# Unread products under the first loads, and half of the first key sum moved to VectorE

## The chip, the cores and the metric

The kernel runs on one core of one Trainium2 chip. What counts is the device time of one execution, from launch to the last output row, in microseconds. The core has a matrix engine (TensorE, PE in the rows), three engines for elementwise work (VectorE = DVE, ScalarE = ACT, GpSimd = POOL) and a queue engine (SyncE = SP) that issues most transfers. Each engine runs its own list of instructions strictly in the order in which the program wrote them and waits on the others through semaphores.

## The reference

Attention over 64 heads with pooled queries, then a capacity-limited expert layer whose tokens are assigned greedily by the gate's scores. Cut to what matters:

```python
def _attn_ref(q, k, v):                       # 8 x 8 heads, 1152 keys of 64
    q_pool = q.reshape(B, H, S // 2, 2, D).mean(axis=3)
    scores = scale * np.matmul(q_pool, k.transpose(0, 1, 3, 2))
    scores = scores - np.max(scores, axis=-1, keepdims=True)
    attn = np.exp(scores)
    attn = attn / (np.sum(attn, axis=-1, keepdims=True) + 1e-09)
    return np.matmul(attn, v)
def _moe_ref(x, w_gate, w1, w2):              # 4608 tokens, 8 experts
    order = np.argsort(-(x @ w_gate).flatten())
    ...                                       # each token to one expert, 576 per expert
    out[mask] = np.maximum(x[mask] @ w1[e], 0.0) @ w2[e]
```

## The kernel before

**Tiling.** Two heads make a pair, 32 pairs in all. For a pair the kernel loads keys (`KD`), queries (`QD`, later `QS`) and values (`VD`) in float32 and splits each into a high and a low float16 part (`KH`/`KL`, `QH`/`QL`, `V16`). The scaling of the split comes from a bound: sums of absolute values per partition (`VM`), added over partitions by TensorE into the bank `mb` (line 537 and after), turned into powers of two by VectorE (`VE`, lines 553 and 555) and into factors by ScalarE (`SC`, `EX`).

Ahead of a pair's exponentials its exact row maxima are needed. TensorE multiplies `QH` with `KH` in chunks (line 684 for the first pair, 693 for later ones) and VectorE reduces each chunk to its maximum (line 687, 696). For the first pair this is done head by head: 15 chunks of 384 keys per head, on five PSUM banks for the first head (`ma`, `av0`, `av1`, the first banks of `sc0` and `sc1`) and on `ma` and `mb` for the second. The maxima are folded (lines 724, 725), transposed by TensorE (line 738) and written as an extra row of `QB` by VectorE (lines 742, 745). Only then can the score products of that head start.

A step of attention (`step`, line 759) takes one head and 128 keys: four score products (line 776) into `sc0` or `sc1`, the exponential by ScalarE into `P` (779), the low part `PM` by GpSimd or VectorE (783), and 15 weighted-value products (793). A pair has 18 steps. After the last pair the expert stage follows; the change doesn't touch it.

**Start of the program.** Transfers of the first two pairs are issued at once. TensorE begins with products of two constant tiles (`ones` and `wide`, 128x128 by 128x512, line 916) that nobody reads: 10 into `av1` (key `wu`) and 13 into `av0` (key `wx`).

**What sets the order.** All attention work is collected as items with engine, function, reads and writes; `Cycle.plan` (line 165) emits an item as soon as all that it needs is emitted, always the one with the smallest due time. Due times are a table by tag and pair: `TAU0` for the first pair, `TAU1` and `TAU2` for the next two, `TAU` for the rest. An engine's list is the order in which its items are emitted.

The lines that the steps below touch: `bounds` (522), where `abk` are the absolute sums of the two key halves of the first pair and `vs` the sums by TensorE; `split` (583); `max_chunk` (674); `fill` and `pads` (483, 496), which clear buffers; and the loop over `wu`, `wv`, `wx`, `wy` (914).

Of the kernel before, what the change touches and what calls it, by code (L numbers as in the profile page):

```python
# [21 lines left out]
AF = mybir.ActivationFunctionType  # L22
OP = mybir.AluOpType
AX = mybir.AxisListType
# [3 lines left out]
M = S // 2  # L28
# [124 lines left out]
class Cycle(Order):  # L153
# [11 lines left out]
    def plan(self):  # L165
# [52 lines left out]
TAU0 = {"abk": [-158.8971, -154.1632], "abs": [-18.36343, -4.432959], "aug": [-83.38275, -166.4732], "augt":  # L218
# [5 lines left out]
        -31.28967, -16.54009, 11.37296, -165.2382, 7.395536, -8.984111, -4.211814], "expb": [-29.09149,  # L224
        -22.94875, -1.956318, -58.58073, -17.31112, 8.70511, -44.15053, -10.60943, -83.61574], "fill":
# [150 lines left out]
def attention(ctx, tc, top, kt, qt, v, wg, w1, x_dram, L, npair=NPAIR):  # L376
    nc = tc.nc
    const = ctx.enter_context(tc.tile_pool(name="att_const", bufs=1))
    psum = ctx.enter_context(tc.tile_pool(name="att_psum", bufs=1, space=PSUM))
    od = Cycle()  # L380
# [7 lines left out]
    ones = const.tile([128, 128], BF, name="ones")  # L388
# [1287 lines left out]
```

## Time and profile before

| what | value |
|---|---|
| runs | 1231.44, 1232.99, 1235.9 us; median 1232.99 |
| the profiled execution | 1237.53 us; span of the trace 1235.8 us |
| busy in the span | PE 1190.0 us (96%), DVE 1018.7 (82%), ACT 972.0 (79%), POOL 901.6 (73%) |
| chain that ended last | PE 77%, DVE 13%, DMA 4%, issue 2%, ACT 2% |

Between the execution's time and its span lie 1.7 us of launch and end. A share of the whole span is an average over stages: the first 24 us, the attention of 32 pairs, the routing and the experts have different limits, and a stage has to be read by itself. In timelines the records of neighbouring products overlap, because the end of a product is modelled; a row with a count gives the time from the first start to the last end.

### The profile page before, as it was taken

The page shows a single profiled execution, that of the slowest core. Times are in us where ns is not written, and L with a number is a line of the kernel's source. Part 1 is how long each engine was busy: PE and PEld are TensorE (multiplying, and loading weights), DVE is VectorE, ACT ScalarE, POOL GpSimd, SP SyncE. Part 2 cuts the span into 40 slices and gives each one's busy share as a digit, 9 for nine tenths or more (in the row PEclk, how much of TensorE's full clock was granted, in tenths as well). Part 3 has the DMA queues.
Part 4 walks back from the last instruction along what each step waited for, and adds up shares of the span by engine and source line. Part 5 has one row for each costly group of instructions (what it writes and reads, how often), then busy time and mean ns, then how long its engine had stood idle before and what let it go on. Part 6 is the DMA issues. An engine that isn't in the chain of part 4 may idle for free.

```text
span 1235.8 us, 38902 instructions
## 1 busy us (share of the span) xinstructions
PE 1190.0 (96%) x15470; PEld 860.7 (70%) x15470; DVE 1018.7 (82%) x2743; ACT 972.0 (79%) x1719; POOL 901.6 (73%) x879
## 2 busy tenths in 40 slices
PE   7899999999999999999999999789999999999998
PEld 2567778778778777777787788465657466575673
DVE  6899899999999999999999995779888898893520
ACT  6979899999899898999999986065876686786751
POOL 6978898898888998888888887044775584675641
PEclk9999999999999999999999999889999999999999
DMA  8666776876776866776876730042453554547401
GB/s 250 151 158 165 186 189 163 196 186 160 191 185 160 193 182 162 195 184 159 197 188 157 180 93 20 20 175 86 129 196 111 159 192 130 171 138 230 120 31 39
DMA packets 131218, 190.83 MB, mean 154 GB/s; under 512 B 50268, under 2 KB 86108, under 8 KB 128732
## 3 DMA queue, kind: packets, MB, share of 16 engines
q1 hardware_dynamic: 117948, 126.75, 38.9%
q0 software_dynamic: 12944, 61.58, 17.5%
q8 instruction: 121, 1.98, 0.7%
q14 instruction: 61, 0.50, 0.1%
q10 hardware_dynamic: 144, 0.02, 0.0%
HBM read 116.41 MB, written 18.87 MB: 109 GB/s over the span
## 4 chain that ended last, share of the span: by engine, by line
PE 77%; DVE 13%; DMA 4%; issue 2%; ACT 2%; POOL 0%; SPq 0%; POOLq 0%; ACTq 0%; DVEq 0%
PE sc L776 20%; PE av L793 18%; PE ph L1561 11%; PE po L1591 11%; PE mb L693 4%; PE ma L693 4%; DVE MX L696 3%; PE av L828 1%; DMA BD<-QH 1%; PE av L840 1%; ACT P L779 1%; DMA W<-in_w_dram,widx 1%; PE po L1597 1%; PE rt L1194 1%; DVE HX L1570 1%
## 5 line engine op out<-in xcount | busy, mean ns | idle before, releaser
L783 POOL TENSOR_TENSOR PM<-P 128x576 f16<-128x576 f32 x508 | 612.4, 1266 | 99.6 <-ACT P L779 48.3
L779 ACT ACTIVATE P<-sc,EX 128x576 f32<-128x576 f32 x576 | 412.6, 739 | 76.0 <-PE sc L776 58.8
L793 PEld LDWEIGHTS <-P 128*128 128x128 bf16 x5760 | 293.0, 98 | 30.0 <-issue 1.9
L793 PE MATMUL av<-V,P 128*128 128x65 f16 (+1 forms) x5760 | 301.2, 192 | 0.0
L793 PE MATMUL av<-V,PM 128*128 128x65 f16 x2880 | 292.8, 194 | 0.0
L793 PEld LDWEIGHTS <-PM 128*128 128x128 f16 x2880 | 263.8, 97 | 0.0
L776 PE MATMUL sc<-QA,KA 128*128 128x288 f16 x1152 | 234.5, 285 | 1.4 <-ACT P L779 1.3
L776 PE MATMUL sc<-QB,KB 65*128 65x288 f16 (+1 forms) x1152 | 235.7, 285 | 0.0
L696 DVE TENSOR_REDUCE MX<-mb 128x1 f32<-128x512 f32 x279 | 190.7, 684 | 27.8 <-PE mb L693 22.7
L696 DVE TENSOR_REDUCE MX<-ma 128x1 f32<-128x512 f32 x279 | 190.6, 683 | 9.8 <-PE ma L693 6.8
L776 PEld LDWEIGHTS <-KA 128*128 128x128 f16 x1152 | 106.2, 97 | 73.1 <-issue 22.7
L1591 PE MATMUL po<-W2H,HX 128*128 128x512 f16 x512 | 155.5, 379 | 0.0
L1561 PE MATMUL ph<-XH,W1H 128*128 128x320 f16 (+1 forms) x512 | 146.2, 286 | 0.7 <-DVE WE L1539 0.3
L1561 PE MATMUL ph<-XL,W1H 128*128 128x320 f16 (+1 forms) x512 | 146.2, 286 | 0.6 <-DVE XL L1455 0.6
L1561 PE MATMUL ph<-XH,W1L 128*128 128x320 f16 (+1 forms) x512 | 145.9, 286 | 0.0
L776 PEld LDWEIGHTS <-KB 65*128 65x128 f16 (+1 forms) x1152 | 112.5, 98 | 29.4
L1591 PEld LDWEIGHTS <-HX 128*128 128x128 f16 x768 | 71.2, 98 | 78.5 <-issue 0.5
L1561 PEld LDWEIGHTS <-W1H 128*128 128x128 f16 x1024 | 97.9, 98 | 30.7 <-issue 6.1
L1613 POOL DMA_INDIRECT out_dram<-OT,idx x40 | 39.2, 980 | 109.1 <-ACT OT L1593 91.2
L693 PE MATMUL ma<-KH,BD 128*128 128x512 f16 x279 | 105.7, 379 | 3.5 <-DVE MX L696 1.3
L693 PE MATMUL mb<-KH,BD 128*128 128x512 f16 x279 | 105.5, 378 | 3.3 <-DVE MX L696 1.4
L1514 POOL TENSOR_TENSOR W2L<-W,W2H 128x512 f16<-128x512 f32 x64 | 73.2, 1159 | 38.5 <-ACT W L1512 34.1
(308 smaller groups left out, 2157.9 us busy)
## 6 DMA issues: line engine op xcount, KB each, us to landing
KD<-in_kt_dram SPq DMA_DIRECT2D x64, 288.0 KB
VD<-in_v_dram SPq DMA_DIRECT2D x32, 576.0 KB
WB<-in_w_dram SPq DMA_DIRECT2D x32, 512.0 KB
QA<-QH SPq DMA_DIRECT2D x128, 72.0 KB
KB<-KH SPq DMA_DIRECT2D x64, 144.0 KB
KA<-KH SPq DMA_DIRECT2D x64, 144.0 KB
KA<-KL SPq DMA_DIRECT2D x64, 144.0 KB
x_dram<-X SPq DMA_DIRECT2D x16, 576.0 KB
```

The costliest lines, as they stand in the source:

```text
L693: od.add(t, "PE", 214, lambda: nc.tensor.matmul(m, BD[i][:, j, :], KH[i][:, 512 * c:512 * c + 512], start=True, stop=True), r=bd + [("KH", ...
L696: od.add(t, "DVE", 597, lambda: nc.vector.tensor_reduce(MX[i][:, j, c:c + 1], m, axis=AX.X, op=OP.max), r=[mk], w=[("MX", i, j, c)], tag=" ...
L776: nc.tensor.matmul(c[:, t, :288], a[i][:rows, s, ks], b[i][:rows, s, 288 * t:288 * t + 288], start=first, stop=not first)
L779: od.add(g + 0.1, "ACT", 624, lambda: nc.scalar.activation(p.rearrange("p (t q) -> p t q", t=2), c[:, :, :288], AF.Exp, scale=EX[n % 3][:, ...
L783: od.add(g + 0.2, en, dur, lock=1, fn=lambda: eng.tensor_tensor(pm, p, hi, op=OP.subtract), r=[("P32", g % NP)], w=[("PM", g % NM)], tag="pm")
L793: nc.tensor.matmul(out, w[:, qs], v, start=kb == 0 and j == 0 and y == 0, stop=kb == NKB - 1 and y == 2, skip_group_check=True)
L828: nc.tensor.transpose(m[:, 128 * z:128 * z + 128], X[u][:, 3 * q + z], ident)
L840: nc.tensor.matmul(av[1][32 * q:32 * q + E, :384], wgs[:, c], XT[q].rearrange("p c t -> p (c t)"), start=True, stop=True)
L1514: od.add(tt, "POOL", 1230, lambda o=lo[p], a=raw[p], h=hi[p]: nc.gpsimd.tensor_tensor(o, a, h, op=OP.subtract), r=[key, hk, sk], w=[(nm + ...
L1561: nc.tensor.matmul(p, a[:, d, fs], b[:, d, qs], start=z == 0, stop=z == 11)
L1591: nc.tensor.matmul(o, a[:, z, q0:q0 + 128], b[:, z], start=z == 0 and y == 0, stop=z == 7 and y == 2)
L1613: st = nc.gpsimd.indirect_dma_start(out=out, out_offset=bass.IndirectOffsetOnAxis(ap=idx[i][:n, c:c + 1], axis=0), in_=OT[ob][:n], in_offs ...
```

## The change

Four edits, and new due times for the first three pairs.

1. The 13 unread products `wx` go; `wu` grows from 10 to 11 and is due before all else.
2. Behind the sums of the first pair's bound stand six unread products into `av1` (tag `wv`).
3. Behind 12 of the 15 chunk products of the first head stands one unread product into the second bank of `sc0`.
4. The absolute sum of the second key half of the first pair is a VectorE reduce (tag `abd`) in place of a ScalarE activation with accumulation.

The core of the diff:

```diff
-TAU0 = {"abk": [-158.8971, -154.1632], ..., "wu": [-17.875, -17.555, ...], "wx": [-4.689, -4.369, ...], ...}
+TAU0 = {"abd": [-140.0], "abk": [-3.247596, -6.270317], ..., "wu": [-300, -299.99, ...], "wv": [-250], ...}
...
-      5, "np": 10, "nm": 10, "stick": 1, "nx": 3, "wu": 10, "pd": [4, 12], "wv": 0, "pd0": [], "pd1": [1, 2, 4, 9, 10,
-      15, 16, 17], "d1": 2.0, "cw1": 0.7, "wx": 13, "wy": 0}
+      5, "np": 10, "nm": 10, "stick": 1, "nx": 3, "wu": 11, "pd": [4, 12], "wv": 0, "pd0": [], "pd1": [1, 2, 4, 9, 10,
+      15, 16, 17], "d1": 2.0, "cw1": 0.7, "wx": 0, "wy": 0}
...
         if n == 0 and not a:
-            for z in range(2):
-                od.add(t, "ACT", 680, lambda z=z: nc.scalar.activation(
-                    VJ[:, :M], KD[n % 2][:, z * M:z * M + M], AF.Abs, accum_out=VM[i][:, 3 * z:3 * z + 1]), ..., tag="abk")
+            od.add(t, "ACT", 680, lambda: nc.scalar.activation(
+                VJ[:, :M], KD[0][:, :M], AF.Abs, accum_out=VM[i][:, 0:1]), r=[("KD", 0, 0)], w=[("VM", i, 0)], tag="abk")
+            od.add(t, "DVE", 680, lambda: nc.vector.tensor_reduce(VM[i][:, 3:4], KD[0][:, M:2 * M], axis=AX.X, op=OP.add, apply_absolute_value=True),
+                   r=[("KD", 0, 1)], w=[("VM", i, 3)], tag="abd")
...
+        if not n and not a:
+            def busy():
+                for _ in range(6):
+                    nc.tensor.matmul(av[1], ones, wide, start=True, stop=True)
+            od.add(t + AT["bs"], "PE", 1280, busy, r=["mb"], w=["av1"], tag="wv")
...
-            od.add(t, "PE", 163, lambda: nc.tensor.matmul(
-                m[:q, :384], QH[i][r, 128 * j:128 * j + q], KH[i][r, 384 * c:384 * c + 384], start=True, stop=True),
-                r=..., w=[mk], tag="mm" + "01"[h])
+            def chunk():
+                nc.tensor.matmul(m[:q, :384], QH[i][r, 128 * j:128 * j + q], KH[i][r, 384 * c:384 * c + 384], start=True, stop=True)
+                if not h and (j, c) not in ((0, 2), (2, 1), (2, 2)):
+                    nc.tensor.matmul(sc[0][:, 1], ones, wide, start=True, stop=True)
+            od.add(t, "PE", 163 if h else 376, chunk, r=..., w=[mk], tag="mm" + "01"[h])
```

What the new table moves is read from the engines' lists. First TensorE where the chunks of the first head begin (`QH_89`, `KH_85`: the first pair; `sc_166`, `av_169` and so on are the PSUM tiles; "waits" names the engines whose semaphores it waits on). Before:

```order
L916 MATMUL av_169<-wide,ones 128x512
L684 LDWEIGHTS QH_89 [waits DVE_49]
L684 MATMUL av_169<-KH_85,QH_89 128x384 [waits Activation_49]
...
L684 MATMUL sc_166<-KH_85,QH_89 128x384
...
L684 MATMUL av_168<-KH_85,QH_89 128x384
...
L684 MATMUL sc_167<-KH_85,QH_89 64x384
...
L684 MATMUL ma<-KH_85,QH_89 128x384
```

And now, from the last of the six products behind the sums:

```order
L566 MATMUL av_169<-wide,ones 128x512
L691 LDWEIGHTS QH_89 [waits DVE_49]
L691 MATMUL sc_166<-KH_85,QH_89 128x384 [waits Activation_49]
...
L693 MATMUL sc_166<-wide,ones 128x512
...
L691 MATMUL av_169<-KH_85,QH_89 128x384
...
L693 MATMUL sc_166<-wide,ones 128x512 [waits DVE_49]
...
L691 MATMUL ma<-KH_85,QH_89 128x384
...
L693 MATMUL sc_166<-wide,ones 128x512
...
L691 MATMUL av_168<-KH_85,QH_89 128x384
```

Between the chunks stand unread products, and the second of them waits for VectorE: it writes the tile `sc_166`, of which VectorE still has to reduce the first bank. Two more of the twelve wait in the same way further down. The chunk products behind a waiting one wait with it.

ScalarE from the first sums on, where `VM` takes the sums, `SC` and `EX` are the factors of the bound and `VQ` takes the square sum of values. Before:

```order
L532 ACTIVATE VJ,VM_126<-QS_124 128x576 [waits DVE_49]
L528 ACTIVATE VJ,VM_126<-KD_119 128x576 [waits DMAHW2_49,Activation_49]
L528 ACTIVATE VJ,VM_126<-KD_119 128x576 [waits DMAHW3_49,Activation_49]
L564 ACTIVATE SC_113<-VE_135 128x2 [waits DVE_49]
L572 ACTIVATE EX_116<-SC_113 128x1 [waits Activation_49]
L573 ACTIVATE EX_116<-VE_135 128x1 [waits DVE_49]
L595 ACTIVATE KH_85<-KD_119,SC_113 128x576
L600 ACTIVATE QS_124<-QS_124,SC_113 128x576 [waits DVE_49]
L595 ACTIVATE KH_85<-KD_119,SC_113 128x576
L598 ACTIVATE KD_119<-KD_119,SC_113 128x576 [waits Activation_49]
L532 ACTIVATE VJ,VQ<-VD_122 128x1152 [waits DMAHW5_49]
```

And now:

```order
L532 ACTIVATE VJ,VM_126<-QS_124 128x576 [waits DVE_49]
L526 ACTIVATE VJ,VM_126<-KD_119 128x576 [waits DMAHW3_49,Activation_49]
L569 ACTIVATE SC_113<-VE_135 128x2 [waits DVE_49]
L600 ACTIVATE KH_85<-KD_119,SC_113 128x576 [waits Activation_49]
L577 ACTIVATE EX_116<-SC_113 128x1
L578 ACTIVATE EX_116<-VE_135 128x1 [waits DVE_49]
L605 ACTIVATE QS_124<-QS_124,SC_113 128x576 [waits DVE_49]
L532 ACTIVATE VJ,VQ<-VD_122 128x1152 [waits DMAHW5_49]
L600 ACTIVATE KH_85<-KD_119,SC_113 128x576 [waits DMAHW2_49]
L603 ACTIVATE KD_119<-KD_119,SC_113 128x576 [waits Activation_49] x2
L532 ACTIVATE VJ,VQ<-VD_123 128x1152 [waits DMAHW6_49]
```

One sum is gone. The first key half is converted directly behind the factors, the second one behind the scaling of `QS` and the square sum of `VD`, and the square sum of the second pair's values has come forward.

On the other lists: VectorE clears the padding of `P` and `PM` (20 small instructions) behind the addition of the two query halves and not ahead of it, makes `ndiag` before that addition and not among the reduces, and reduces one chunk of the second head ahead of the extra row of the first. GpSimd makes the index table for `ndiag` at the start and clears the two `BD` buffers behind the low parts of the keys. SyncE issues the fourth `QA` copy and the second weight load later, and the second of the pair-1 copies of `AU` comes 14 transfers behind the first and no longer directly behind it. Behind the first few pairs all lists are the same as before.

## Rows read from the trace of the kernel before

**Rows 1.** windows by stage; width, busy us (count) per engine, PEclk, DMA, GB/s

```profile
0.00:24.00 24.00, 16.09 (x45) 4.58 (x46) 14.11 (x54) 16.18 (x30) 14.51 (x24) 1.00 0.92 270
24.00:36.00 12.00, 11.04 (x109) 5.89 (x108) 8.78 (x23) 10.19 (x18) 10.05 (x9) 1.00 0.37 116
36.00:50.00 14.00, 12.23 (x140) 8.03 (x141) 13.42 (x23) 12.56 (x21) 14.00 (x14) 1.00 0.59 164
...
150.00:175.00 25.00, 25.00 (x420) 20.04 (x418) 22.81 (x45) 22.86 (x39) 22.14 (x22) 1.00 0.69 170
```

**Rows 2.** timeline of TensorE, 0 to 75 us; start, us, what [idle before]

```profile
3.34 2.30 PE L916 MATMUL av<-wide,ones 128*128 128x512 bf16 x5 [3.34 <-DVE floor L396]
...
21.31 1.25 PE L916 MATMUL av<-wide,ones 128*128 128x512 bf16 x5
...
24.43 0.42 PE L776 MATMUL sc<-QA,KA 128*128 128x288 f16 x2
```

**Rows 3.** timeline of ScalarE, 0 to 75 us

```profile
8.03 0.68 ACT L528 ACTIVATE VJ<-KD 128x576 bf16<-128x576 f32 x1
...
9.25 0.20 ACT L564 ACTIVATE SC<-VE 128x2 f32<-128x2 f32 x1 [0.45 <-DVE VE L553]
...
17.58 0.20 ACT L568 ACTIVATE SC<-VE 128x1 f32<-128x1 f32 x1 [0.71 <-DVE VE L558]
...
22.50 0.19 ACT L532 ACTIVATION_READ_ACCUMULATOR VJ<-QS 128x1 f32 x1
...
25.13 0.74 ACT L779 ACTIVATE P<-sc,EX 128x576 f32<-128x576 f32 x1 [2.44 <-PE sc L776]
...
29.20 0.20 ACT L564 ACTIVATE SC<-VE 128x2 f32<-128x2 f32 x1
```

**Rows 4.** timeline of VectorE, 0 to 75 us

```profile
3.15 0.11 DVE L501 MEMSET P<- 128x64 f32 x2
...
3.90 0.45 DVE L501 MEMSET PM<- 128x32 uint32 x10
...
5.62 0.76 DVE L588 TENSOR_TENSOR QS<-QD 128x576 f32<-128x576 f32 x1 [1.27 <-DMA QD<-in_qt_dram]
...
11.64 0.56 DVE L687 TENSOR_REDUCE MX<-av 128x1 f32<-128x384 f32 x1 [1.32 <-PE av L684]
...
18.98 0.54 DVE L687 TENSOR_REDUCE MX<-ma 128x1 f32<-128x384 f32 x1
19.44 0.54 DVE L687 TENSOR_REDUCE MX<-sc 128x1 f32<-128x384 f32 x1
...
23.85 0.27 DVE L745 SCALAR_TENSOR_TENSOR QB<-mb,CB,ndiag 5x64 f16<-5x64 f32 x1
...
36.44 0.27 DVE L745 SCALAR_TENSOR_TENSOR QB<-mb,CB,ndiag 5x64 f16<-5x64 f32 x1
```

**Rows 5.** chain of waits, 0 to 110 us; start, us, what

```profile
18.47 2.25 PE av L916 x5
...
21.42 1.03 DVE MX L687 x2
...
51.63 4.13 PE av L793 x135
```

**Rows 6.** windows of 2 us late in the kernel, same columns

```profile
780.00:782.00 2.00, 1.06 (x9) 0.49 (x6) 1.54 (x8) 0.00 (x0) 0.00 (x0) 1.00 0.00 0
782.00:784.00 2.00, 1.61 (x12) 1.06 (x13) 1.40 (x7) 0.00 (x0) 0.00 (x0) 0.58 0.00 0
```

**Rows 7.** timeline of GpSimd, 0 to 80 us

```profile
25.95 7.78 POOL L783 TENSOR_TENSOR PM<-P 128x576 f16<-128x576 f32 x7 [3.26 <-ACT P L779]
...
49.20 3.63 POOL L783 TENSOR_TENSOR PM<-P 128x576 f16<-128x576 f32 x3
```

**Rows 8.** timeline of the SyncE queue, 0 to 60 us

```profile
16.30 1.10 SPq L642 DMA_DIRECT2D KA<-KL  x2
```

**Rows 9.** tile QS, 0 to 60 us: its GpSimd transfers, issue to landing

```profile
DMA to landing us min/median/max: 5.4/5.5/5.6
```

More of the change, by code (lines that the diff above doesn't have):

```diff
@@ L272 @@
[L272 removed]
[5 rows of a table removed]
[L278 to L281 removed]
[7 rows of a table removed]
[L289 removed]
[4 rows of a table removed]
[L294 removed]
+TAU0 = {"abd": [-140.0], "abk": [-3.247596, -6.270317], "abs": [-22.78447, -0.5571336], "aug": [-49.20042, -63.65756], "augt":
[5 rows of a table added]
+        [-101.5423, -18.87479, -31.42721, -95.43, 4.982884, -83.49272, -8.005609, -143.5481, 16.64426], "expb":
+        [-22.75529, -40.03387, -77.62868, -79.1448, -30.53657, -2.177917, -18.52933, -29.97288, -77.77242],
+        "fill": [17.15927, -27.82857, -23.76563, -16.43919, -137.43, -18.75261, -69.09106, 10.14575, 16.42628,
[12 rows of a table added]
+        0.8312891, -116.2708, -51.32051, -17.92582, 24.11002], "qkb": [-41.59464, -18.72518, -6.461611,
[7 rows of a table added]
@@ new lines @@
+TAU1 = {"abs": [-3.567419, -2.884223, -16.47506], "aug": [-11.41736], "augd": [-49.99403, 9.887361], "augt":
[5 rows of a table added]
+        "expa": [-34.35519, -39.44459, 6.983353, -9.443917, 11.10978, -0.8630265, 18.51459, -9.853134,
+        -9.48902], "expb": [-14.63436, 2.394361, -12.9281, -32.8816, 14.86851, 17.76486, 19.58756, -32.18436,
+        4.203153], "fold": [-67.2291], "kd": [-27.68356, -16.33625, -60.78294], "kh": [-22.2747, -18.85138],
+        "kl": [-141.8632, -19.41825], "ld": [-38.975, -38.325], "ldq": [-40.925], "ldv": [-39.625], "ldw":
[4 rows of a table added]
+        -169.846, -56.01792, -8.813194, -73.22199, -51.50618, -77.50039], "mre": [-76.34698, -9.109999,
[3 rows of a table added]
+        -7.830657, 3.022983, -113.6533, 26.66848], "qkb": [-75.88482, -6.136093, 3.949606, 7.30092, -37.77197,
+        -137.5603, -47.86212, -75.17828, 22.27336], "ql": [-12.73021], "rc": [4.795404, -7.290796], "sc":
+        [-108.1857], "scv": [-9.175092], "spr": [-113.9553, -75.84297, -3.197515, -1.441281, 1.480276,
+        0.05174173, -24.02959, -30.81659, -22.04622, -74.7476, -10.09451, -70.50754], "vd": [-10.90741,
+        -8.755863], "vh": [-120.5216, -53.9324], "vl": [-38.48606, -9.518776], "vs": [-145.6367, -50.742],
+        "vsh": [-16.1903], "wsq": [11.81812], "x": [3.479598, -116.5068]}
@@ new lines @@
+TAU2 = {"abs": [-23.4975, -25.08641, -26.23569], "aug": [-14.60879], "augd": [-37.69011, -17.43024], "augt":
[5 rows of a table added]
+        [-51.9563, -87.83583, 11.56729, 11.74051, 4.501346, 17.61292, 8.607434, -26.29048, -67.10155], "expb":
+        [4.700961, -115.0573, -24.42258, 11.60432, 13.4284, -4.90717, 4.748511, -105.6011, -6.529959], "fold":
+        [-9.159572], "kh": [-31.96585, -24.85616], "kl": [-132.7912, -32.1933], "ld": [-27.96813, -84.05359],
+        "ldq": [-139.8815], "ldv": [-53.46438], "ldw": [-78.02513], "me": [-15.49425, -10.66331, -2.929244],
[7 rows of a table added]
+        [3.485547, 5.850303, 7.472656, -68.70809, 16.64328, 17.42214, 19.19644, 21.93961, 27.13442], "qkb":
[4 rows of a table added]
+        -116.044], "vsh": [-45.67116], "wsq": [10.11431], "x": [34.10587, -12.73376]}
@@ L683, in max_chunk @@
             r, q = slice(64 * h, 64 * h + 64), 128 if j < 4 else 64
-            od.add(t, "PE", 163, lambda: nc.tensor.matmul(
-                m[:q, :384], QH[i][r, 128 * j:128 * j + q], KH[i][r, 384 * c:384 * c + 384], start=True, stop=True),
-                r=[("QH", i)] + [("KH", i, z) for z in ((0,), (0, 1), (1,))[c]], w=[mk], tag="mm" + "01"[h])
+            def chunk():
+                nc.tensor.matmul(m[:q, :384], QH[i][r, 128 * j:128 * j + q], KH[i][r, 384 * c:384 * c + 384], start=True, stop=True)
+                if not h and (j, c) not in ((0, 2), (2, 1), (2, 2)):
+                    nc.tensor.matmul(sc[0][:, 1], ones, wide, start=True, stop=True)
+            od.add(t, "PE", 163 if h else 376, chunk, r=[("QH", i)] + [("KH", i, z) for z in ((0,), (0, 1), (1,))[c]], w=[mk], tag="mm" + "01"[h])
             od.add(t, "DVE", 463, lambda: nc.vector.tensor_reduce(MX0[:q, h, j, c:c + 1], m[:q, :384], axis=AX.X, op=OP.max),
```

31 lines of the change are left out of this document (removed), and 99 rows, old and new, of tables (TAU0, TAU1, TAU2).

## The prediction

> **What bounds the kernel now.** I read the windows by stage first. In the attention proper TensorE is busy in 25.00 of 25 us (150 to 175), and the change touches nothing there. In the first 24 us it is busy in 16.09, part of it with products that nobody reads, and up to 50 us it still idles 1 to 2 us a stage [rows 1]. So the change is worth what it moves the start of the first pair's scores, provided that nothing later takes it back.
>
> Then the timelines of the first 25 us, engine by engine. TensorE runs at the lower of its two clocks there: five 512-column products take 2.30 us from 3.34 on and still 2.25 at 18.47, but 1.25 at 21.31 [rows 2, 5], that is 0.45 and 0.25 each: 1.2 GHz, then 2.4. (The PEclk column reads 1.00 for this stage [rows 1]; the lengths of the products contradict it.) VectorE reduces the 15 chunks of the first head between 11.64 and 22.45, 10.8 us, though two neighbours start only 0.46 apart, 18.98 and 19.44 [rows 4, 5]: 15 x 0.46 = 6.9, so 3.9 us are waits for slow TensorE and for other entries. The extra row of QB ends at 24.12, 1.67 behind the last reduce, the first score product starts at 24.43, and ScalarE, which ended its own work at 22.69, starts the first exponential at 25.13 after 2.44 us of waiting [rows 2 to 4]. What ends last in this stage is the row maximum of the first head.
>
> **The change part by part.**
>
> *The sum on VectorE.* ScalarE's second key sum starts at 8.03 and ends with its readout about 8.81; the factors follow at 9.25 [rows 3]. Now VectorE does it: its addition of the query halves ends at 6.38, the 20 small clears that were moved behind it took 1.20 (3.15 to 4.35), and a reduce of 576 columns is not in the trace. A 384-column reduce takes 0.56 [rows 4]; in proportion to columns 0.84 at most, 0.56 at least, and I take 0.75. That ends at 6.38 + 1.20 + 0.75 = 8.33, and the other half on ScalarE at 8.03. The factors come 0.48 earlier, at 8.77. Bounds: 0.78 earlier if VectorE is done before 8.03; 1.5 later if clears and reduce take twice as long and more.
>
> *Unread products ahead of the sums.* Eleven at 0.45 from 3.34 are over at 8.3, under the loads and the sums, so they delay nothing. Six more follow the sums at about 8.6: 1.5 us at the upper clock, to 10.1; 2.7 at the lower one, to 11.3. The first key half is converted straight behind the factors (0.20 and, as for the equally wide exponential, 0.74 [rows 3]), ready at 9.7. I take the upper clock from some point among these products, and the first chunk at 10.1. Bounds: 9.7 and 11.3.
>
> *Chunks.* At the upper clock an unread product is 0.25 and a chunk of 384 columns 0.19, together 0.44, just under the 0.46 of a reduce; VectorE sets the pace from 10.5 on, once it has made the limits of the exponent. The second key half is converted later in ScalarE's list, behind the scaling of QS and a square sum, about 12.7, when five chunks have kept VectorE busy till 12.8: no wait, or 0.3. Three unread products wait for a reduce of the tile sc0, with the next chunk queued behind them, and VectorE waits for that chunk: 0.15 each, 0.5 in all (nothing at best, a full 0.46 each at worst). With 0.3 for the two small instructions of the value bound the 15 reduces end at 10.5 + 6.9 + 0.3 + 0.5 = 18.2 in place of 22.45, 4.2 earlier.
>
> *To the first score.* One reduce of the second head now stands ahead of the extra row: 18.2 + 0.46 + 1.67 = 20.3; the first scores run from 20.4 to 21.0. They also need the copies of the keys' low part, issued at 16.30 and after [rows 8], now about as late. When these land the trace doesn't show. Their bounds are at once and the 5.5 us of the slowest transfers in this stage [rows 9], 22.2; I take 20, since the queue holds mostly small copies by then.
>
> *ScalarE becomes the last.* From the factors to the end of its work before the first exponential it takes 9.25 to 22.69, 13.44, of which 0.71 is a wait [rows 3] that the new order has no reason for. The same instructions are in the new list: 8.77 + 12.7 = 21.5. So the first exponential starts at 21.5, not at 21.0 and not at 25.13: 3.6 us gained, and the score products' lead of 0.5 hides small errors above.
>
> *What follows.* Two scores then lie ready, so the first five exponentials follow each other at 0.74 or less, 3.7, to the second pair's factors at 25.2; before it was 29.20, 4.07 after the first exponential [rows 3]. That makes 4.0. GpSimd's first low part PM waited for the exponential at 25.95 [rows 7]; it now has the two clears of BD behind the keys' low parts and starts about 22.5, 3.45 earlier. It falls back by 0.6 against the rest, but its last PM of the pair ends at 52.83, 2.9 before the products that use it end at 55.76 [rows 5, 7]. The extra row of the second head ended at 36.71 [rows 4]; from there VectorE is busy 13.42 of 14 us [rows 1] and moves as a block. SyncE's second AU copy, now behind 14 transfers, is wanted half a pair later. I cost these, and the new order of the two pairs behind, at nothing, with 1.5 us either way.
>
> *Sum.* 4.0 us. The profiled execution took 1237.53 (span 1235.8 and 1.7 around it), 4.5 above the median of 1232.99; 1237.5 - 4.0 = 1233.5 for a like execution, and 1229.0 for the median.
>
> *A rule weighed.* Late in the kernel the granted clock read 1.00 from 780 to 782 with TensorE busy in 1.06 of 2 us, and 0.58 in the next two [rows 6]: a fall to the lower level behind an engine that worked half of the time. The Trainium skill (TensorE: Matmul & The Clock Gate, Part 1: The HAM clock gate) has the clock fall after idleness, and says that the point of release moves from run to run. By its words the thin stretch behind the last unread product, about 17.5 to 22.3, would be safe, and the sum stands; by the row it need not be, and that is rival 1. What it says of the release would make the lift late in some runs: rival 2. The measurement decides, so both keep a chance.
>
> **The rivals.**
>
> 1. *The clock falls at the handover.* Between 17.5 and 22.3 TensorE has only short chunks, one transpose and two scores. For: the fall at 782 [rows 6]. Against: before the change the score products at 24.43 ran at the upper clock, two of 288 columns in 0.42, right behind the 1.67 us up to 24.12 in which TensorE had next to nothing [rows 2, 4]. A score of four 288-column products is 0.56 at the upper clock, 1.1 at the lower; about three run before the clock returns, 1.7 more, of which ScalarE's 0.74 per exponential hides a third: 1.2 lost, 1230.2.
> 2. *The clock rises late.* If the six products behind the sums still run at 0.45, the first chunk starts at 11.3, and five chunks with their unread products take 0.8 each to 15.3 (five reduces after 12.8 become 15.4): 2.6 late, 1.0 of it hidden by the wait for the second key half and ScalarE's lead. The gain is 2.4: 1230.6.
> 3. *The copies land late.* If the low keys need 5.5 us, the first score is at 22.2 and the first exponential at 22.9: gain 2.6, 1230.4. For: the transfers are busy in 0.92 of the stage [rows 1]. Against: these are small and on chip.
> 4. *The gain is given back* between 57 and 100 us, where transfers and VectorE alternate as last: 0.5 left, 1232.5.
> 5. *Slower: the clock does not come back.* Chunks of 64 rows, scores spaced by ScalarE and no unread products any more could leave TensorE at the lower level through 24 to 36 us, where it is busy 11.04 of 12 at the upper one [rows 1]. Twice that is 22: 11 more, less 4.0 gained: 1240, and 1234.5 if only 6 of the 12 us are slow. It decides against the change once the clock is low for over 4.4 us there (4.0 of loss at 0.92 a us). Against: before 21.31 the clock rose among a mixture of chunks and unread products too.
> 6. *More than forecast.* The new order of the second and third pair fills some of the idle 1.8 us of 36 to 50 [rows 1] and as much behind: 1227.0.
>
> **How the numbers follow.** Forecast 0.44, rivals 1 to 3 together 0.28, rival 4 0.08, rival 5 0.08, rival 6 0.12. Time 1229.0. The forecast's own range is 1227.5 to 1230.5; rivals 1 to 3 add up to 1231, rival 4 reaches 1232.5, rival 6 1226. The range 1226.0 to 1232.8 leaves out rival 5 and tails. The 0.3% that a measurement tells from no change are 3.7 us, 1229.3: the forecast is faster by that in six of ten, rival 6 always, rivals 1 to 3 in one of five: 0.26 + 0.12 + 0.06 = 0.44. Slower 0.08. Within 0.3%: 0.48.
>
> **What would show it.** Right: five of the first unread products at 0.45 and chunks of the first head at 0.25 or less apart from 10 us on; VectorE's 15 first-head reduces between 10.5 and 18.5; the first exponential at 21.5 straight behind ScalarE's own work, without a wait for a score; the second extra row ending at 32.5 to 33; all later lines some 4 us earlier, and the busy time of TensorE from 150 on unchanged. Wrong: products at 0.45 after 12 us; an exponential that waits for a score whose keys come by a copy; PEclk or product lengths at the lower level after 18; or a lead of 4 us at 33 that is gone at 100.

## The result, and the profile after

The changed kernel takes 1243.62 us in the median (1241.0 to 1244.69, 5 runs), the kernel before 1232.99 (1231.44 to 1237.23, 5 runs): a ratio of 1.0079, 95% interval 1.0063 to 1.0095. By the medians it is 10.6 us slower, where I had forecast 4.0 faster. The profiled execution of it took 1244.69 us, with a span of 1242.9.

First the windows by stage, with the columns of [rows 1], and five narrower ones. PEclk is the column to follow.

```profile
0.00:24.00 24.00, 17.83 (x57) 5.76 (x57) 15.48 (x58) 15.07 (x28) 14.53 (x24) 0.83 0.95 267
24.00:36.00 12.00, 11.35 (x42) 4.25 (x40) 5.46 (x13) 7.28 (x13) 7.62 (x7) 0.50 0.28 85
36.00:50.00 14.00, 13.20 (x99) 7.83 (x99) 8.32 (x18) 8.31 (x14) 9.56 (x9) 0.62 0.49 127
...
14.00:15.00 1.00, 0.24 (x2) 0.10 (x1) 1.00 (x4) 0.97 (x4) 1.00 (x1) 1.00 1.10 325
15.00:16.00 1.00, 0.96 (x4) 0.25 (x3) 0.73 (x2) 1.00 (x2) 1.00 (x5) 0.94 1.08 282
16.00:17.00 1.00, 1.00 (x4) 0.24 (x3) 0.78 (x2) 0.97 (x3) 1.00 (x3) 0.50 1.07 191
...
46.00:47.00 1.00, 1.00 (x6) 0.64 (x5) 1.00 (x2) 0.18 (x1) 0.74 (x1) 0.70 0.80 249
...
85.00:90.00 5.00, 3.23 (x13) 1.84 (x13) 3.24 (x9) 1.96 (x5) 2.37 (x3) 0.76 0.37 95
```

The granted clock falls to 0.50 late in the window from 15 to 16 (0.94 of it: at 15.9) and is back in the one from 46 to 47 (at about 46.6). For 31 us TensorE runs at 1.2 GHz. From 24 to 36 it is as busy as before, 11.35 against 11.04 of 12 us [rows 1], and that is what deceives: in it TensorE makes 42 products, where it made 109 before. From 150 to 175 it is busy in 25.00 of 25 us as before [rows 1]. A second fall, at 85 to 90, comes with another thin stretch.

TensorE's timeline of the same execution around the first fall and at the first score:

```profile
2.10 4.27 PE L925 MATMUL av<-wide,ones 128*128 128x512 bf16 x11 [2.10 <-DVE wide L390]
7.74 1.46 PE L566 MATMUL av<-wide,ones 128*128 128x512 bf16 x6
...
13.92 0.32 PE L691 MATMUL av<-KH,QH 64*128 64x384 f16 x1
15.04 0.38 PE L693 MATMUL sc<-wide,ones 128*128 128x512 bf16 x1 [0.80 <-DVE MX L696]
15.35 0.33 PE L691 MATMUL av<-KH,QH 64*128 64x384 f16 x1
...
15.94 0.52 PE L691 MATMUL sc<-KH,QH 64*64 64x384 f16 x1
16.39 0.61 PE L693 MATMUL sc<-wide,ones 128*128 128x512 bf16 x1
...
23.23 0.66 PE L785 MATMUL sc<-QA,KA 128*128 128x288 f16 x2
```

The early products do what they were put there for: six in 1.46, 0.24 each, so the upper clock is there by 7.74, while before it came at about 21 [rows 2]. Then an unread product into tile sc0 stands for 0.80 us behind a reduce, the clock falls at 15.9, and the next unread product takes 0.61 in place of 0.39. Half a score, two products of 288 columns, takes 0.66 where [rows 2] has 0.42.

The stand alone does not bring the fall. `i1_burst` (below), whose program is the same up to here, has the same stand, and three unread products behind it still run at 0.39; its clock falls at 17.7:

```profile
15.16 0.38 PE L695 MATMUL sc<-wide,ones 128*128 128x512 bf16 x1 [0.80 <-DVE MX L702]
...
16.92 0.39 PE L695 MATMUL sc<-wide,ones 128*128 128x512 bf16 x1
```

ScalarE and VectorE, again of the changed kernel's execution:

```profile
8.11 0.20 ACT L569 ACTIVATE SC<-VE 128x2 f32<-128x2 f32 x1 [0.45 <-DVE VE L553]
20.29 0.19 ACT L456 ACTIVATION_READ_ACCUMULATOR VJ<-WB 128x1 f32 x1
24.41 0.74 ACT L788 ACTIVATE P<-sc,EX 128x576 f32<-128x576 f32 x1 [3.93 <-PE sc L785]
25.91 0.74 ACT L788 ACTIVATE P<-sc,EX 128x576 f32<-128x576 f32 x1 [0.77 <-PE sc L785]
```

```profile
6.91 0.71 DVE L528 TENSOR_REDUCE VM<-KD 128x1 f32<-128x576 f32 x1
9.85 0.56 DVE L696 TENSOR_REDUCE MX<-sc 128x1 f32<-128x384 f32 x1
20.10 0.56 DVE L696 TENSOR_REDUCE MX<-ma 128x1 f32<-128x384 f32 x1 [0.65 <-PE ma L691]
22.49 0.27 DVE L754 SCALAR_TENSOR_TENSOR QB<-mb,CB,ndiag 5x64 f16<-5x64 f32 x1
42.54 0.27 DVE L754 SCALAR_TENSOR_TENSOR QB<-mb,CB,ndiag 5x64 f16<-5x64 f32 x1
```

Up to the first exponential the change still leads, 24.41 against 25.13 [rows 3]. Behind it each exponential waits for a score, and the second extra row ends at 42.8, 6.1 later than before [rows 4]. ScalarE ended its own work at 20.5 and then waited 3.93 us for the first score. How lead and loss run can be read from the starts of ScalarE's exponentials, here by number in the program (us, one profiled execution each; the kernels below before are experiments):

| kernel | 1st | 6th | 10th | 18th | 28th | 37th | last (576th) | TensorE at the lower clock, once it had risen, to 100 us |
|---|---|---|---|---|---|---|---|---|
| before | 25.1 | 30.5 | 37.8 | 50.6 | 68.6 | 84.2 | 769.6 | never (rose at about 21) |
| after | 24.4 | 32.9 | 44.5 | 59.0 | 76.1 | 94.4 | 779.2 | 15.9 to 46.6, and in 85 to 95 |
| e1_own_bank | 23.5 | 32.0 | 42.7 | 56.4 | 74.1 | 90.8 | 775.4 | 19.8 to 40.2 |
| e2_hold | 22.5 | 28.1 | 35.2 | 48.9 | 67.6 | 85.9 | 771.8 | in 75 to 85 |
| e4_before_no_wx | 24.3 | 32.9 | 43.7 | 56.6 | 74.6 | 90.2 | 775.2 | rose only at about 42 |
| i1_burst | 26.6 | 32.0 | 39.2 | 52.9 | 71.7 | 87.3 | 773.9 | 17.7 to 24.5 |

The changed kernel is 0.7 ahead at the first, 8.4 behind at the 18th, 10.2 behind at the 37th, and 9.6 at the last: the whole loss arises before 95 us and is carried along. That is close to the difference of the medians (10.6). The spans differ by 7.1 only, since the profiled execution of before lay 4.5 above its median; from the last exponential to the end it took 466.1 us, the changed kernel 463.7.

### The profile page after: what moved, and what is told of

It reads as the page before. It is cut to its first block, busy times and chain, and to the rows that moved or that the text cites. A ratio compares the mean times of both kernels' runs of the same rounds, so it can differ in the third digit from the quotient of the medians.

```text
span 1242.9 us, 38912 instructions
## 1 busy us (share of the span) xinstructions
PE 1199.7 (97%) x15476; PEld 864.9 (70%) x15476; DVE 1019.8 (82%) x2744; ACT 970.7 (78%) x1717; POOL 902.2 (73%) x879
## 4 chain that ended last, share of the span: by engine, by line
PE 72%; DVE 11%; DMA 7%; ACT 5%; issue 3%; POOL 1%; SPq 1%; POOLq 0%; ACTq 0%; DVEq 0%
PE sc L785 21%; PE av L802 18%; PE ph L1570 9%; PE po L1600 7%; PE mb L702 5%; PE ma L702 4%; DMA W<-in_w_dram,widx 2%; DVE MX L705 2%; DMA XG<-XB 1%; PE av L837 1%; DMA BD<-QH 1%; PE av L849 1%; ACT SQ L1537 1%; ACT W L1521 1%; DVE GE L1197 1%
## 5 line engine op out<-in xcount | busy, mean ns | idle before, releaser
L802 PEld LDWEIGHTS <-P 128*128 128x128 bf16 x5760 | 294.4, 98 | 30.3 <-issue 2.2
L785 PE MATMUL sc<-QA,KA 128*128 128x288 f16 x1152 | 238.2, 288 | 1.5 <-ACT P L788 1.1
L785 PE MATMUL sc<-QB,KB 65*128 65x288 f16 (+1 forms) x1152 | 239.2, 289 | 0.0
L705 DVE TENSOR_REDUCE MX<-ma 128x1 f32<-128x512 f32 x279 | 190.6, 683 | 10.1 <-PE ma L702 7.2
```

Source lines behind the costliest of these rows:

```text
L705: od.add(t, "DVE", 597, lambda: nc.vector.tensor_reduce(MX[i][:, j, c:c + 1], m, axis=AX.X, op=OP.max), r=[mk], w=[("MX", i, j, c)], tag=" ...
L785: nc.tensor.matmul(c[:, t, :288], a[i][:rows, s, ks], b[i][:rows, s, 288 * t:288 * t + 288], start=first, stop=not first)
L802: nc.tensor.matmul(out, w[:, qs], v, start=kb == 0 and j == 0 and y == 0, stop=kb == NKB - 1 and y == 2, skip_group_check=True)
```

## The experiments

My theory was that TensorE's clock makes the loss: it falls at the stand of 0.80 us and stays low. Rival A: the new order loses by itself. Rival B: the fall comes from the thin stretch at the handover to the scores, not from the stand. Rival C: the unread products cost time.

**The stand taken away: e1_own_bank.**

```diff
-                nc.tensor.matmul(m[:q, :384], QH..., KH..., start=True, stop=True)
                 if not h and (j, c) not in ((0, 2), (2, 1), (2, 2)):
-                    nc.tensor.matmul(sc[0][:, 1], ones, wide, start=True, stop=True)
+                    nc.tensor.matmul(m, ones, wide, start=True, stop=True)
+                nc.tensor.matmul(m[:q, :384], QH..., KH..., start=True, stop=True)
```

> The changed kernel, but each of the twelve unread products among the first head's chunks goes into the chunk's own bank, ahead of the chunk, instead of into tile sc0: it then waits for nothing that the chunk does not wait for anyway, and the 0.80 us in which TensorE stood behind a reduce (14.25 to 15.04) go. My theory (the loss is TensorE's clock, and it fell at that stand): products of 512 columns stay at 0.25 and less through 16 to 19 us, the clock column is 1.00 over 16 to 46, the first exponential starts at 21.5 to 22.5, and the time is 1228 to 1231. Rival A (the new order of the work loses by itself): the clock stays up and the time is 1236 or more all the same. Rival B (the thin stretch at the handover lets the clock fall, not the stand): no stand of 0.80, but products at 0.45 again from some point between 17 and 24 on, and 1235 to 1243.

Measured: 1242.28 against 1232.76 for before, ratio 1.0071 (1.0055 to 1.0087). Its profiled execution lay 3 us below that median. TensorE's timeline and, behind it, its windows (columns as above):

```profile
16.93 0.33 PE L693 MATMUL ma<-KH,QH 64*128 64x384 f16 x1
18.20 0.32 PE L693 MATMUL ma<-KH,QH 64*128 64x384 f16 x1 [0.94 <-DVE MX L696]
...
20.14 0.48 PE L693 MATMUL mb<-KH,QH 64*128 64x384 f16 x1 [0.66 <-DVE QB L754]
22.37 0.64 PE L785 MATMUL sc<-QA,KA 128*128 128x288 f16 x2 [1.75 <-DMA KA<-KL]
```

```profile
18.00:20.00 2.00, 0.94 (x3) 0.32 (x3) 1.78 (x6) 1.97 (x6) 1.51 (x3) 0.94 1.04 213
20.00:22.00 2.00, 0.48 (x1) 0.00 (x0) 1.11 (x3) 0.66 (x2) 1.98 (x2) 0.50 1.05 225
...
40.00:44.00 4.00, 3.17 (x30) 1.96 (x28) 2.79 (x5) 1.69 (x3) 3.64 (x3) 0.97 0.82 208
```

Without the stand the clock holds through 16 and falls at 19.8, in the handover, as rival B has it. So the stand isn't needed for the fall; that it makes it earlier (15.9 and 17.7 with it, 19.8 without) rests on one execution each. And a second thing shows: the first score then waits 1.75 us for the copy of the keys' low part.

**The handover filled: e2_hold**, that kernel and

```diff
+                if h:
+                    seen.append(z)
+                    for _ in range({1: 3, 2: 3, 3: 1, 4: 1}.get(len(seen), 0)):
+                        nc.tensor.matmul(av[1], ones, wide, start=True, stop=True)
```

> As the run with the products in the chunk's own bank, and eight more unread products (3, 3, 1, 1) behind the first four chunks of the second head, where TensorE waits for the row maximum and the extra row. My theory: no better than without them if the stand of 0.80 us was the cause, 1228 to 1231, at most 0.5 later for the last two. Rival B (the handover lets the clock fall): only this one of the two keeps the clock, and it is 5 us or more faster than the other. Rival A: 1236 or more with the clock up.

Measured: 1237.52 (1232.74 to 1244.36), ratio 1.0040 (1.0021 to 1.0060). Its windows:

```profile
18.00:20.00 2.00, 1.66 (x8) 0.61 (x8) 1.50 (x5) 1.97 (x6) 2.00 (x3) 1.00 1.05 220
...
24.00:36.00 12.00, 10.40 (x107) 5.94 (x107) 8.53 (x22) 10.62 (x19) 11.39 (x11) 1.00 0.39 105
...
75.00:80.00 5.00, 3.18 (x43) 2.00 (x40) 4.49 (x10) 1.61 (x3) 3.56 (x4) 0.90 0.66 146
80.00:85.00 5.00, 5.00 (x78) 3.79 (x77) 3.24 (x6) 4.22 (x8) 1.93 (x2) 0.75 0.32 72
```

The clock holds, and in 24 to 36 us TensorE makes 107 products in 10.40 us where the changed kernel makes 42 in 11.35. The tenth exponential is 9.3 us earlier than in the changed kernel, the last 7.4. So the clock at the handover makes a large part of the loss: by the last exponential 7.4 of 9.6, by the medians about half (a ratio of 1.0040 where the change has 1.0079). The rest of the profiled execution's loss is not the handover's, and the sign that I had set for rival A, 1236 or more with the clock up, did come. The lead over before, 2.6 us at the first exponential, is 0.6 at the 19th (55.71 against 56.35) and a loss of 1.7 at the 37th. Where it goes shows at the turns to the second and to the third pair. First SyncE's timeline in e2_hold, TensorE's behind it, and SyncE's in the kernel before:

```profile
46.70 0.58 SPq L454 DMA_DIRECT2D WB<-in_w_dram  x1
47.33 0.46 SPq L647 DMA_DIRECT2D QA<-QH  x1
```

```profile
54.96 0.41 PE L791 MATMUL sc<-QA,KA 128*128 128x288 f16 x2 [1.62 <-DMA QA<-QH]
```

```profile
49.34 0.60 SPq L642 DMA_DIRECT2D QA<-QH  x1
```

At the turn to the second pair TensorE is ready at 53.34 and waits 1.62 us for a copy of queries; before it waited there for nothing but ScalarE, 0.40. By the semaphores' updates in the trace, the last copy that this score needs is the one issued at 47.33, straight behind a weight load, and it lands at 54.83. Before, the last one is issued at 49.34 and lands at 54.38, and TensorE comes to that score only at 55.6. So TensorE is 2.2 us earlier and the copy is not. The weight load in front of it is the second one, which the change issues later; that moving it back would help was not tested. The turn to the third pair, TensorE and VectorE:

```profile
78.27 0.28 PE L763 MATMUL mb<-ident,CM 128*9 128x128 f32 x1 [1.08 <-DVE CM L743]
```

```profile
78.58 0.34 DVE L764 TENSOR_SCALAR AU<-mb,EX 9x128 f16<-9x128 f32 x1 [0.37 <-DMA KA<-KH]
```

Here VectorE writes the extra row (`AU`) at 78.58, where before did at 78.51: what was left of the lead, 1.0 at the 28th exponential, is gone by then. The profile names a copy for VectorE's wait, but the transpose that makes `mb` ends at 78.55, and that one waited 1.08 for VectorE itself. (So the wait for the copy of the queries that the expectation of f1 below puts at 79 is the one at the first turn.) Then the clock falls, at 79.1, and the 37th exponential is 1.7 behind.

The twelve executions of this kernel differ by 11.6 us, and their mean granted clock goes with the time: 0.995 at 1232.74, 0.992 at 1238.02, 0.982 at 1244.36. A line through all twelve has 0.35 us of time per us at the lower clock (that is twice 1 minus the mean clock, times the span), with a correlation of 0.95. That places nothing: before's nineteen on the same chip follow their clock too (0.38, correlation 0.72), and the one profiled execution here has 3.4 us at the lower clock up to the last exponential and 19.2 behind it. The changed kernel's five all lie at 0.981 to 0.984, which suits a long fall in each, though only one was profiled. In the best of the twelve the held order only draws level with before.

**What the unread products of before are worth: e4_before_no_wx** (`"wx": 13` becomes `"wx": 0`).

> The kernel before without its 13 unread products between 16 and 23 us. My theory (these held up, or brought back, the clock ahead of the first scores): the first 25 us get no longer, but the clock is low through most of 24 to 46 as in the changed kernel, and the time is 1238 to 1246, 5 to 12 more than before. Rival A and C (the clock is not what decides): 1229 to 1234.

Measured: 1237.78, ratio 1.0034 (1.0021 to 1.0048). From TensorE's timeline:

```profile
23.13 0.66 PE L776 MATMUL sc<-QA,KA 128*128 128x288 f16 x2
...
41.43 0.63 PE L693 MATMUL ma<-KH,BD 128*128 128x512 f16 x1
42.68 0.39 PE L693 MATMUL mb<-KH,BD 128*128 128x512 f16 x1 [0.61 <-DVE QB L745]
```

The first score comes 1.3 earlier than in the kernel before, at the lower clock (0.66 against 0.42, [rows 2]); a product of 512 columns still takes 0.63 at 41.43 and 0.39 at 42.68. 13 products without a reader are worth 5.0 us. Taking them out, which is one edit of the change, costs about half as much as the whole change.

**Order alone: e3_bare**, the changed kernel without the unread products among the chunks and with one behind the sums.

> The changed kernel without its unread products among the chunks and with one instead of six behind the sums; the order, the sum on VectorE and the eleven early ones stay. My theory: nothing keeps the clock up between 9 and 24, so it falls by 15 at the latest and the loss stays, 1240 to 1246. Rival C (the unread products cost TensorE the time that the change was to gain): 1232 or less. Rival A: 1240 or more too, but with the clock up over 24 to 46.

Measured: 1241.14, ratio 1.0060 (1.0042 to 1.0077). The clock falls in the window from 8 to 10 (0.65) and is back in 36 to 40 (0.58); the last exponential starts 5.5 later than before. So the unread products aren't what costs most of the time (rival C): without them 8.4 us remain. Whether they cost the other 2 can't be told, since the intervals overlap. Nor do they, as the change places them, keep the clock.

**A dose in the low stretch: i1_burst**, the changed kernel and twelve unread products behind the second head's second chunk (`{2: 12}` in the loop of e2_hold). This and the runs below were made on other chips, on which the kernel before took 1253.90 (i1, i2, i3), 1259.54 (f1 to f4) and 1253.13 (h2, g1, g3); the additional time lies behind the last exponential (f3_before_abd: the last at 769.3, near the 769.6 of before, but a span of 1257.2), so their ratios stand against before on the same chip and the starts of exponentials can be laid side by side.

> The changed kernel with one addition: twelve unread products of 512 columns behind the second of the second head's chunks, ahead of the first score, where TensorE is at the lower clock; at 0.45 each they take 5.4 us, of which about 1 lies beside the making of the extra row. Theory (the clock decides; such products lift it where the chunks and scores of 24 to 46 us do not): products of 288 columns at the upper clock from 26 to 30 us on instead of 46.7, the first exponential 4 us later than in the changed kernel, the tenth at 39 to 42 instead of 44.5, and the time 1238 to 1241 by 1243.6. Rival (the clock comes back at a time of its own, whatever TensorE does): lower clock to about 46, tenth exponential at 48 or later, 1246 to 1249.

Measured: 1259.62, ratio 1.0048 (1.0027 to 1.0068). TensorE's timeline:

```profile
21.41 4.27 PE L699 MATMUL av<-wide,ones 128*128 128x512 bf16 x12
25.62 0.33 PE L693 MATMUL mb<-KH,QH 64*128 64x384 f16 x1
25.88 0.42 PE L791 MATMUL sc<-QA,KA 128*128 128x288 f16 x2
```

The clock is back within these products (0.50 to 24, 0.98 over 24 to 36) and stays. They put the first score 2.7 us later than in the changed kernel, and the tenth exponential comes 5.3 earlier. So the clock came back with these products, 22 us ahead of its return in the changed kernel; the rival of a return at a time of its own had 46.

**More hold: i2_hold_more** (5, 5, 2, 2).

> The run with the clock held through the handover, with 14 instead of eight unread products there (5, 5, 2, 2). That run's executions lay between 1232.7 and 1244.4. Theory (in some executions the clock falls at the handover all the same, since eight products are just enough): fewer late executions, the highest under 1240, the median 1234 to 1236 by a kernel before at 1232.8. Rival (the late executions come from falls further on, at 79 us): the median stays at 1237 to 1239 and the spread too.

Measured: 1259.18 (1252.21 to 1265.75), ratio 1.0043 (1.0024 to 1.0062). In the profiled execution, the fastest, the clock holds to the turn at 78 and falls there, as in e2_hold; the 28th exponential leads by 2.0, and the last is level with before. The spread stays, as the rival has it, but before spreads over 10.8 us itself on this chip; what the other executions lost, no profile here shows.

**The old order with the clock up early: f2_before_early, h2_old_order_held, i3_old_order_5.** The first gives before ten products ahead of the sums and twelve among the chunks in their own banks; h2 adds six behind the sums and the sum on VectorE; i3 is h2 with five of the 13 `wx`.

> The kernel before in its own order, with its ten early unread products all ahead of the sums and twelve more among the chunks of the first head, each into the chunk's own bank; its 13 products at the handover stay. Theory (the clock decides): TensorE reaches the upper clock by about 12 us instead of 20.6 and keeps it; the 15 reduces of the first head end at 20 to 21 instead of 22.45, the first exponential starts at 23 to 24, bounded by the copy of the keys' low part, and the time is 1231 to 1232, 1 to 2 below before. Rival (the unread products are in the way of the chunks at the lower clock): first exponential at 25 or later, 1233 to 1235.

> The kernel before in its own order of the pairs, with the sum of the second key half on VectorE, the ten early unread products all ahead of the sums, six behind them, twelve among the first head's chunks (each into the chunk's own bank), and the 13 of the handover kept. Theory (the clock decides, and the old order of the later pairs gives nothing back): TensorE at the upper clock from 6 to 8 us on without a fall before the last pair ends, the first exponential at 22 to 23, and a lead of 2 to 3 us over the kernel before that is still there at the last exponential: a ratio of 0.9975 to 0.9985. Rival (the lead is given back at the second pair, whatever its order): under 1 us of lead at the 28th exponential, ratio 0.9995 to 1.002.

> The old order with the clock held from the start, with five instead of 13 unread products at the handover (those straight ahead of the transpose). In the run with 13, five of them stood ahead of the last two chunks of the first head for 1.2 us at the upper clock, and the first exponential came at 24.0. Theory: the last chunks come 1 us or more earlier, the first exponential at 22 to 23, the lead of 2 to 3 us stays to the last pair, ratio 0.997 to 0.999. Rival (with five products the clock falls at the handover in some or all executions): ratio 1.002 to 1.007 and a wide spread.

Measured: f2 1265.99, ratio 1.0051 (1.0033 to 1.0068); h2 1257.65 (1248.29 to 1262.96), 1.0032 (1.0009 to 1.0056); i3 1259.04, 1.0042 (1.0021 to 1.0062). In f2 (the profiled execution is its slowest, 1270.77) the clock falls at 9.4 in a wait of 1.43 for the keys, comes back at 26.4, and the chunks with their products crawl: first exponential at 30.3; it falls again from 36.7 to 43.5. In i3 it falls at 18.0 and the last exponential is 10.0 late. In h2 it holds from the first chunk to the last exponential, and the lead of 1.2 at the first exponential (24.0) is 1.9 at the last (767.8). Yet the median is slower. TensorE in h2 and in i3 at the first score:

```profile
20.15 1.25 PE L925 MATMUL av<-wide,ones 128*128 128x512 bf16 x5
...
23.27 0.42 PE L785 MATMUL sc<-QA,KA 128*128 128x288 f16 x2
```

```profile
19.87 2.32 PE L924 MATMUL av<-wide,ones 128*128 128x512 bf16 x5
...
23.84 0.66 PE L784 MATMUL sc<-QA,KA 128*128 128x288 f16 x2
```

The windows of h2 up to its last exponential and behind it:

```profile
0.00:767.80 767.80, 752.87 (x12164) 583.54 (x12165) 687.54 (x1383) 682.17 (x1176) 658.86 (x608) 1.00 0.69 171
767.80:1256.90 489.10, 449.56 (x3330) 281.70 (x3326) 333.24 (x1362) 290.49 (x542) 241.62 (x271) 0.97 0.38 122
```

So what makes this execution slow (5.5 above the median of before) lies behind the attention, in stages that the edits don't touch: 489.1 us at 0.97 of the clock, against 481.9 and 483.7 in g1 and g3 on the same chip. Its executions follow the mean clock too (0.993 at 1248.29, 0.983 at 1262.96). Whether a start that is 1.9 earlier brings on these later falls, or they are chance, no run here shows.

**The sum on VectorE alone: f3_before_abd.**

> The kernel before with the one edit that the absolute sum of the first pair's second key half is made by VectorE. Theory: the factors come 0.5 to 0.8 earlier, but the first chunk stands behind five unread products that end at 11.10 whatever the factors do, so the time is that of before within 0.5, 1232.3 to 1233.3. Rival: the sum by VectorE is what costs (it delays the reduces or the clears): 1234 or more.

Measured: 1258.87, ratio 0.9994 (0.9977 to 1.0012). The exponentials start 1.2 earlier from the first (24.0) to the 37th (83.1), and 0.4 earlier at the last (769.3). I had overlooked that the five products in the way stand behind the sums and move with them. This part of the change does no harm that shows; 1.2 us is less than this measurement can tell.

**Mixed tables: f1_hold_old12, f4_keys_first, g1_hold_old1, g3_hold_old12**, all e2_hold with `TAU1`, or `TAU1` and `TAU2`, of before. f4 also moves a square sum behind the scalings of the keys, which brings its first score from 22.90 to 22.86, that is nothing.

> The run with the clock held through the handover, with the due times of the second and third pair (TAU1, TAU2) as in the kernel before. That run led the kernel before by 2.4 us at the sixth exponential and was 1.6 behind at the 37th, 1.1 of it given back at the turn to the second pair and 2.6 at a fall of the clock at 79 us behind a wait for the QA copy. Theory (the new order of the second and third pair gives the lead back): the lead at the 19th exponential is 2 us or more, no fall between 50 and 100, time 1229 to 1231. Rival (the first pair's order, or the transfers under it, gives it back whatever follows): the lead is under 1 us by the 28th exponential and the time 1232 to 1236.

> As the held clock with the old second and third pair, and in the first pair ScalarE makes its square sum of the values (1.15 us) behind the scalings of the keys instead of ahead of them, so that GpSimd's low keys and their copies are issued about 1.2 us earlier. Theory (with the clock up, the first score waits for that copy: 0.60 us in the held run, 1.75 in the one without hold): first score at 20.8 instead of 21.8, first exponential 0.9 earlier, 0.5 to 1.0 below the run without this edit. Rival (the extra row or ScalarE's own work binds by then): the same within 0.3.

> The run with the clock held through the handover (3, 3, 1, 1 unread products), with the due times of the second pair alone (TAU1) as in the kernel before; the mix with the third pair's too had put three sums of that pair ahead of the first exponentials on ScalarE, which is not so here. Theory (the changed kernel's order of the second pair gives the lead back): the lead over the kernel before is 2 us or more at the 28th exponential and the clock does not fall between 50 and 100; ratio 0.998 to 0.9995. Rival (the first pair's new order itself gives it back): lead under 1 us there, ratio 1.002 to 1.005.

> As the run with the old due times of the second pair, and those of the third pair (TAU2) as in the kernel before too, but for the third pair's three sums on ScalarE, which keep the changed kernel's. Theory: as that run up to the 36th exponential, and no wait for the QA copy at the turn to the third pair, so 0 to 1.5 us better behind it. Rival: the same as that run within 0.3.

Measured: 1280.55 (ratio 1.0166, 1.0148 to 1.0184), 1281.52 (1.0179, 1.0159 to 1.0198), 1264.50 (1.0096, 1.0074 to 1.0118), 1262.74 (1.0072, 1.0056 to 1.0087). They don't answer their question. The due times of three pairs are one set: mixed, they put sums whose loads come late ahead of the exponentials (f1 and f4), as ScalarE's timeline of f1 shows,

```profile
26.11 0.68 ACT L532 ACTIVATE VJ<-QS 128x576 bf16<-128x576 f32 x1 [6.69 <-DMA QS<-in_qt_dram]
...
34.88 1.16 ACT L532 ACTIVATE VJ<-VD 128x1152 bf16<-128x1152 f32 x1 [6.04 <-DMA VD<-in_v_dram]
```

and g1 and g3, which start well (23.0 and 21.7), are 7.6 and 7.7 us behind before at the 18th exponential, with falls of the clock in both (three of 3.4 us from 18.5 on; 36.5 to 46.7). Whether the new order of the second pair by itself gives the lead of e2_hold back stays open. No version measured here beats the kernel before.

## Why the prediction was wrong

*The step that failed* is "I take the upper clock from some point among these products", with the 0.44 per chunk and unread product and the scores "from 20.4 to 21.0" that rest on it. The rise was right, and earlier than said. What I didn't carry on is that it must also be kept: the sum has no term for the clock once it is up, and it was down from 15.9 to 46.6. Rival 5 had the mechanism, "could leave TensorE at the lower level", with 24 to 36 us as its place and 0.08 as its chance; it came at 15.9 and lasted 30.7. My argument against it, that the clock "rose among a mixture of chunks and unread products too", left out that all 13 of these unread products stood between 16.5 and 22.6 us, next to the first score; in e4_before_no_wx, without them, it rose only at about 42. The same goes for rival 1, which I priced at 1.2 us with the words that "the clock returns" after three scores. In five profiles (after, e1, e3, e4, i3) it did not return with the scores: each had its first weighted-value products at 37.0 to 39.0 and the upper clock 2.4 to 8.2 us after that.

The rule weighed: the Trainium skill (TensorE: Matmul & The Clock Gate, Part 1: The HAM clock gate) has activity release the clock. By that and by the busy column, 11.35 of 12 us, it should have been released in 24 to 36 us; it was not, and the measurement decides. That section of the Trainium skill also has the point of release move from run to run. The traces agree: the eleven early products start at 2.10 in the changed kernel, in i1_burst and in g1_hold_old1 and take 4.27, 4.85 and 3.88 us. The point of the fall moves as well, 15.9 and 17.7 in the first two. In the changed kernel and in e1_own_bank it comes with thin work (0.24 in the us from 14 to 15, 0.94 in the two from 18 to 20), so the row of [rows 6] was the better guide, as rival 1 said.

*The sum on VectorE*: 0.71 for the reduce (forecast 0.75), factors at 8.11 (8.77), 1.1 earlier than before. Right, and better.

*Unread products ahead of the sums*: the eleven start at 2.10 rather than 3.34, because `wide` is ready then. The first chunk is at 9.18 (10.1).

*Chunks*: forecast 10.5 to 18.2, measured 9.85 to 20.6. The waits of the three products were to be 0.15 each, "a full 0.46 each at worst": they were 0.38, 0.80 and 0.20. The one at 15.04 is above the worst case: the reduce it waited for (14.44) stood itself behind two others and two small instructions in VectorE's list.

*First score*: forecast 20.4. With the clock held it started at 21.80 and waited for the copy KA<-KL, not for the extra row (20.5). I had taken 20 for the landing of these copies; it was 21.7, 5.6 after the issue at 16.05. That is rival 3 with its 5.5 us. Its gain of 2.6 is also e2_hold's lead at the first exponential, but by luck: the rival had that exponential at 22.9, a lead of 2.2, and it came at 22.5.

*ScalarE becomes the last*: forecast, its own work to 21.5. It ended at 20.5, and the first exponential then waited for its score. So this term, which was to hide small errors above, hid none: with the clock held the copy is last, in the changed kernel the slow chunks.

*What follows*: I had 4.0 us stay to the end. Even with the clock held the lead was 0.6 at the 19th exponential: rival 4, earlier than placed, and there by a copy rather than "where transfers and VectorE alternate". The new order of the next pairs, costed "at nothing, with 1.5 us either way", gives no gain back to keep: 2.6 gained, 2.0 of it gone by the first turn, the rest by the second, and 1.7 lost behind the fall there. With the clock up at the handover, e2_hold's profiled execution is 2.2 behind before at its last exponential, and the median is 4.8 behind.

*The rivals together*: I added rivals 1 to 3 up to 1231. Their losses of 1.2, 1.6 and 1.4 make 1233.2, outside the range that I gave; it changes nothing in the step that failed.

*The other end*: "all later lines some 4 us earlier, and the busy time of TensorE from 150 on unchanged": the second half held.

Of the 9.6 us at the last exponential, 7.4 go with the clock up to and through the handover (after less e2_hold, one execution each), and 2.2 are left in e2_hold with its fall at 79. Why e2_hold's median is behind by more than that stays open.

## What to carry to other kernels

When a change takes away or moves work that nobody reads, ask first what TensorE's clock was in that stretch and which products kept it there, and give its fall a price: the length of the stretch at half rate, not that of the gap. A busy share says nothing of speed; read the products per window and the length of one known product beside it. An early rise is worth nothing if the clock falls again in a thin stretch between it and the real work, so fill the last stretch ahead of the real work first, and let a filler write only what its neighbour waits for anyway. And ask of a lead what else must come earlier for it to last: here a copy behind a weight load did not. Holding the clock gave back what losing it had cost, in part; it made no version faster than the kernel before.

## What the runs showed that was not expected

- TensorE stayed at the lower clock for 30.7 us though busy in 21.34 of 22.60 us from 24 to 46.6; twelve products of 512 columns brought it back within 3.1 us (21.41 to 24.5).
- PEclk reads 1.00 up to the first change on record: in before and in e4_before_no_wx it does so through about 21 and 42 us, in which products of 512 columns have their lower-clock lengths (0.45 apart, 0.63 for a single record; 0.25 and 0.39 at the upper clock).
- One kernel's executions differ by 11.6 us (e2_hold), and their mean granted clock goes with the time; before's nineteen on the same chip differ by 6.3.
- Behind the last exponential, where all these kernels are the same, the profiles take some 20 us more on other chips (span less last exponential: 460.5 to 466.1 in the first six, 480.6 to 489.1 in the ten others).
